# Mixing stage of a gMLP-and-attention kernel: three accumulations opened on six blocks, the last two blocks after all three, and one operand prepared earlier

## The chip, the cores and the metric

The kernel runs on one core of a Trainium2 chip. A core has TensorE (PE, the matmuls; PEld are its weight loads), VectorE (DVE), ScalarE (ACT), GpSimd (POOL), and SyncE (SP), which issues most of the transfers. Each engine works through its own list of instructions in order and waits on semaphores for the others. The metric is device microseconds of one execution. Times inside the profile are us from the start of the span.

## The reference

```
xn = layernorm(x)                                   # x: 2048 x 512
s  = attention(xn, k_cache, v_cache, wq, wo)        # 32 heads of 128, the last 512 keys
z  = gelu(xn @ w_in)                                # w_in: 512 x 1376
z1, z2 = z[:, :688], layernorm(z[:, 688:])
g  = w_sp @ z2 + b_sp[:, None]                      # w_sp: 2048 x 2048, the "mixing"
out = x + s * silu((z1 * g) @ w_out)                # w_out: 688 x 512
```

All in float32.

## The kernel before

A float32 product is made of three matmuls. Each operand is split into a high half (a cast to fp32r on ACT) and a low half (whole minus high half, by `rest`, L59, on DVE or POOL); the three are high by high, high by low, low by high.

The program has three stretches: attention together with the z1 products (to about 1450 us), the z2 products with their gelu and layernorm (to about 1511 us), and then the mixing product w_sp @ z2 and the projection. The change lies where the second stretch meets the third.

**The z2 loop (L929 to L943).** It walks the 16 row blocks of z2 in the order `ZO` = 8, 9, 0, 1, 10, 11, 2, 3, 12, 13, 4, 5, 14, 15, 6, 7. At position `pos` it first splits the normed pair of rows that ended two positions before (`z_split`: cast L812 on ACT, low half L59 on POOL), then makes the products of this row block for both halves of the 688 columns, with gelu (L787, ACT) and statistics (L788, DVE); `z_norm` closes a layernorm for each pair (L794 on DVE, then L74, L75 and two L801 on POOL), and `z_apply` (L806, ACT, one for each row block of the pair) applies it one position later. Each position also runs `step(t)` with t = pos - 16.

**Slots.** The mixing product is done by a seven-product scheme on half-size blocks for each of the 8 row pairs. A slot (r, k) is one of these products: eight blocks along the contraction, three matmuls each, 24 matmuls (L870) into one bank `ps`. The operand that moves is a pair of z2 row blocks (`b`), the stationary one a prepared row of w_sp (`x8`, printed as x). Slots 0 to 3 are P2 of rows 0 to 3, slots 4 to 7 are P1 of rows 0 to 3. P2 moves B21, which is made of the z2 rows 8 to 15; its blocks seven and eight are rows 14 and 15, which stand at positions 12 and 13 of `ZO` and are split at position 15 (t = -1). P1 moves B11; its blocks seven and eight are rows 6 and 7, positions 14 and 15, applied at t = 1 and split at t = 2.

**Operands.** `prep(n)` prepares the stationary operand of slot n: a cast of 128x1024 on ACT (L855) and its low half on DVE (L59, with x in its names). prep(0) and prep(1) stand at t = -6 and t = -4; from then on `step(t)` starts with prep(t + 2). `step` then runs the events put down for t: `t_diff` (L884, DVE, in pairs) and `t_split` (L889 on ACT, L59 with b in its names on DVE) make the combinations of z2 that later slots move. The rows of w_sp come by `load_halves` (L828, issued by SP): P2 rows 2 and 3 at t = -4, P1 rows 0 and 1 at t = 0, P1 rows 2 and 3 at t = 2. All operands and loaded rows take turns in the eight buffers of the pool `xp`.

**The slot loop (L1097).** For each t it evicts slot t - 1 (P2: nothing; P1: L990 on ACT, L991 and L975 on DVE), runs step(t), and then products(t).

Of the kernel before, what the change touches and what calls it, by code (L numbers as in the profile page):

```python
# [23 lines left out]
NB = FH // 2  # L24
# [16 lines left out]
def mixer_kernel(ctx: ExitStack, tc: tile.TileContext, x, wh, w_in, w_sp, b_sp, w_out, out):  # L41
# [218 lines left out]
    def fetch_x(w, k):  # L260
        X[w][k] = block()
        nc.sync.dma_start(X[w][k].bitcast(F32), xd[w, k])
# [89 lines left out]
    def z1_product(i, n, between=lambda: None):  # L352
        ps = ps_acc.tile([P, 512], F32, name="ps_a") if n or i >= T8 else ps_step.tile([P, 512], F32, name="ps_3")
        zmm(ps[:, :NB], i, n, range(2))
        between()
        zmm(ps[:, :NB], i, n, range(2, NC))
        return ps
# [255 lines left out]
    n, t = 0, 28  # L613
    for p in range(4):
        seq, store = later_x(p)
        for k, (f, ks) in enumerate(seq):
            t = max(t + 2, 30 + 13 * n // 5)
# [43 lines left out]
    ps = ps_step.tile([P, 512], F32, name="ps_3")  # L661
# [9 lines left out]
    ps = ps_step.tile([P, 512], F32, name="ps_3")  # L671
# [4 lines left out]
    ps = ps_acc.tile([P, 512], F32, name="ps_a")  # L676
# [18 lines left out]
    for t in range(T0, T1):  # L695
# [30 lines left out]
        if t in DRAIN:  # L726
            ps = z1_product(*DRAIN[t])
# [21 lines left out]
    ps = z1_product(*LAST[-1])  # L749
# [5 lines left out]
    RP = NT // 2  # L755
# [14 lines left out]
    def hilo(k, j, pool=None):  # L770
        if pool is not None:
            HL[k, j] = blk(pool)
        return tuple(HL[k, j][:, a, :, :NB] for a in range(2))
# [5 lines left out]
    def z_product(i, n):  # L779
        last = i in ZO[-2:]  # L780
        zps[i, n] = (ps_step if last else ps_acc).tile([P, 512], F32, name="ps_3" if last else "ps_a")
        zmm(zps[i, n][:, :NB], i, n, range(NC))

    def z_gelu(i, n):
        if n == 2:
            zst[i] = stats.tile([P, 2, 6], F32, name="stz")
        nc.scalar.activation(zt(i)[:, n - 2], zps[i, n][:, :NB], AF.Gelu_apprx_tanh)  # L787
        nc.vector.bn_stats(zst[i][:, n - 2, :], zt(i)[:, n - 2])  # L788

    def z_norm(pos):  # L790
        g, j = divmod(pos, 2)
        if j == 0:
            zmv[g] = stats.tile([P, 2, 2], F32, name="mvz")
        nc.vector.bn_aggr(zmv[g][:, j, :], zst[ZO[pos]])  # L794
        if j == 1:
            r = stats.tile([P, 2], F32, name="rz_r")
            tmp = stats.tile([P, 2], F32, name="rz_t")
            rsqrt(zmv[g][:, :, 1], r, 2, tmp)
            for k in range(2):
                t, mean, rs = zt(ZO[pos - 1 + k]), zmv[g][:, k, 0:1], r[:, k:k + 1]  # L800
                nc.gpsimd.tensor_scalar(tmp[:, k:k + 1], mean, rs, -1.0, op0=OP.mult, op1=OP.mult)  # L801
                zn.setdefault(pos, []).append((t, tmp[:, k:k + 1], rs))

    def z_apply(pos):
        for t, shift, rs in zn.pop(pos, ()):
            nc.scalar.activation(t, t, AF.Identity, bias=shift, scale=rs)  # L806

    def z_split(pos):
        i = ZO[pos - 1]
        hi, lo = hilo("B21" if i >= RP else "B11", i % RP // 2, br)  # L810
        whole = Z[i // 2][:, :, 0, :NB]
        nc.scalar.copy(hi, whole)  # L812
        rest(nc.gpsimd, lo, whole, hi)
# [6 lines left out]
    NS = len(SLOTS)  # L820
    WHEN = {s: n for n, s in enumerate(SLOTS)}

    rows, s1, ops, bank = {}, {}, {}, {}
# [22 lines left out]
    def prep(n, engine):  # L846
        r, k = SLOTS[n]
        if k in ("P2", "P1"):
            src = rows[k, r // 2][:, r % 2]
        else:  # L850
            a11, a12, a21, a22 = a_blocks(r)
            src = {"P6": a11, "P5": s1[r], "P7": a21, "P3": a12, "P4": a22}[k]
        op = ops[n] = x8([P, 2, RP, P])
        hi, lo = (op[:, a].rearrange("p c t -> p (c t)") for a in range(2))
        nc.scalar.copy(hi, src)  # L855
        rest(engine, lo, src, hi)

    MOVING = {"P1": "B11", "P2": "B21", "P6": "T2", "P5": "T1", "P7": "T3", "P3": "B22", "P4": "T4"}

    def products(n):  # L860
        r, k = SLOTS[n]
        if k == "P4":
            bank[r, k] = bank.pop((r, "P7"))
        else:
            bank[r, k] = pp.tile([P, 512], F32, name="ps", bufs=6)
        ps, op = bank[r, k][:, :NB], ops.pop(n)
        for c in range(RP):
            rh, rl = (t[:, c % 2] for t in hilo(MOVING[k], c // 2))
            for m, (a, b) in enumerate(((op[:, 0, c], rh), (op[:, 0, c], rl), (op[:, 1, c], rh))):
                nc.tensor.matmul(ps, a, b, start=k != "P4" and c == 0 and m == 0,  # L870
                                 stop=c == RP - 1 and m == 2, skip_group_check=True)
# [25 lines left out]
    V, G = nc.vector, nc.gpsimd  # L897

    def step(t):
        if 1 < t + 2 < NS:  # L900
            prep(t + 2, V)
        for f, args in ev.get(t, ()):
            f(*args)
# [25 lines left out]
    for pos, i in enumerate(ZO):  # L929
        if pos > 2 and pos % 2:  # L930
            z_split(pos - 2)
        for n in (2, 3):
            z_product(i, n)
            z_gelu(i, n)
        z_norm(pos)
        z_apply(pos - 1)
        if pos == 5:
            for k in ((0, 1), (1, 1)):
                fetch_x(0, k)
        t = pos - NT  # L940
        if t in (-6, -4):
            prep(t // 2 + 3, nc.vector)
        step(t)  # L943
    left.close()
# [35 lines left out]
    def evict(r, k):  # L980
        if k == "P2":
            return
        ps = (bank[r, k] if k == "P7" else bank.pop((r, k)))[:, :NB]
        v = us[r][:, 3 * NB:4 * NB] if r in us else None
        if k == "P1":
            if r % 4 == 0:
                t = blk(br, F32).rearrange("p a c f -> p (a c f)")
                U.update({r + n: t[:, n * ZW:n * ZW + NB] for n in range(4)})
            c = bank.pop((r, "P2"))[:, :NB]
            nc.scalar.copy(U[r], ps)  # L990
            nc.vector.tensor_tensor(c, c, U[r], op=OP.add)  # L991
            gate(r, 0, c)
        elif k == "P6":
            nc.vector.tensor_tensor(U[r], ps, U[r], op=OP.add)
        elif k == "P5":
            nc.vector.tensor_tensor(v, ps, U[r], op=OP.add)
        elif k == "P7":
            g = pp.tile([P, 512], F32, name="ps_f")[:, :NB]
            nc.vector.tensor_tensor(g, ps, v, op=OP.add)
            gate(r + RP, 1, g)  # L1000
        elif k == "P3":
            nc.vector.tensor_tensor(ps, ps, v, op=OP.add)
            gate(r, 1, ps)
        else:
            nc.vector.tensor_tensor(ps, ps, U[r], op=OP.add)
            gate(r + RP, 0, ps)
# [90 lines left out]
    for t in range(NS):  # L1097
        if t:
            evict(*SLOTS[t - 1])
        step(t)  # L1100
        products(t)
    evict(*SLOTS[NS - 1])
    for t in (NS, NS + 1):
        for f, args in ev.get(t, ()):
# [57 lines left out]
```

## Time and profile before

| what | value |
|---|---|
| median of 3 runs (lowest, highest) | 1793.61 us (1790.58, 1795.43) |
| the profiled execution | 1795.06 us, its span 1793.2 us |
| PE busy | 1770.9 us, 99% of the span |
| DVE, POOL, ACT busy | 1484.6, 1260.9, 1184.5 us |
| mean granted clock of TensorE | 0.996 |
| L870, products of the slots | 1344 matmuls, from 1511.1 to 1727.0 us |

PE is busy nearly all the time, so an idle stretch of PE, or a stretch at a lower granted clock, is what can be had. A matmul's duration overlaps the next one's, so the pace is read from starts and counts and not from durations.

### The profile page before, as it was taken

To read this page: it belongs to the slowest core of one execution; us is meant where nothing else is said; L and a number is where in the kernel's file an instruction comes from. 1 tells how busy PE (TensorE), PEld (TensorE's weight loads), DVE (VectorE), ACT (ScalarE), POOL (GpSimd) and SP (SyncE) were. 2 spreads that over 40 slices of the span, in tenths; PEclk is the share of its full clock that TensorE was granted. 3 is DMA by queue.
4 is the path that set the end of the run, shared out by engine and by line. 5 is a ranking of instruction groups with operands and counts; after the bars stand their busy time and mean duration, and the time that the engine had idled before them with its cause. 6 is when DMAs were issued, how large, how long until landed. Compare 5 with 4: busy or idle time off the path is not lost.

```text
span 1793.2 us, 28567 instructions
## 1 busy us (share of the span) xinstructions
PE 1770.9 (99%) x8460; PEld 1516.4 (85%) x8460; DVE 1484.6 (83%) x2442; ACT 1184.5 (66%) x2634; POOL 1260.9 (70%) x1204
## 2 busy tenths in 40 slices
PE   8999999999999999899999999999999999999999
PEld 7888888888888887688888888888888999999997
DVE  5689988989898988788888888888889646787776
ACT  4777777777777776577777777777777546543333
POOL 2798898898898987678888888888888425000033
PEclk9999999999999999999999999999999999999999
DMA  5588887987888989787787777777778752555487
GB/s 189 182 246 233 244 264 230 265 253 232 256 252 240 268 233 285 237 262 229 221 233 221 224 222 233 221 220 222 230 221 256 213 193 87 196 183 175 146 243 212
DMA packets 181164, 402.12 MB, mean 224 GB/s; under 512 B 24080, under 2 KB 61200, under 8 KB 161808
## 3 DMA queue, kind: packets, MB, share of 16 engines
q1 hardware_dynamic: 176400, 394.66, 74.2%
q10 hardware_dynamic: 4608, 5.64, 0.9%
q8 instruction: 66, 1.08, 0.3%
q14 instruction: 90, 0.74, 0.1%
HBM read 233.74 MB, written 166.46 MB: 223 GB/s over the span
## 4 chain that ended last, share of the span: by engine, by line
PE 88%; DMA 5%; DVE 3%; POOL 2%; ACT 1%; issue 1%; SPq 1%; ACTq 0%; DVEq 0%; POOLq 0%
PE ps_a L450 14%; PE ps L870 12%; PE ps L67 12%; PE ps L65 12%; PE ps L66 12%; PE ps_a L517 6%; PE ps_a L515 6%; PE ps_a L516 6%; PE ps_a L67 2%; PE ps_a L65 2%; PE ps_a L66 2%; DMA p_dram<-pL 1%; DMA pL<-p_dram 1%; PE ps_f L65 1%; PE ps_f L67 1%
## 5 line engine op out<-in xcount | busy, mean ns | idle before, releaser
L59 POOL TENSOR_TENSOR pT_l<-pL,pT_h 128x512 fp32r<-128x512 f32 x507 | 657.2, 1300 | 189.0 <-ACT pT_h L507 179.0
L479 ACT ACTIVATE prob<-ps,nm 128x512 f32<-128x512 f32 x512 | 354.0, 691 | 338.8 <-DVE nm L477 331.1
L539 DVE SCALAR_TENSOR_TENSOR sacc<-ps,sums,sacc 128x512 f32<-128x512 f32 x496 | 370.2, 747 | 129.9 <-PE ps L67 124.4
L450 PE MATMUL ps_a<-x,x 128*128 128x512 f32 x1302 | 377.3, 390 | 5.7 <-DMA x<-x_dram 5.6
L488 DVE STREAM_TRANSPOSE pL<-prob 128x512 f32<-128x512 f32 x512 | 359.4, 702 | 4.1 <-ACT prob L479 4.1
L477 DVE TENSOR_REDUCE nm<-ps 128x1 f32<-128x512 f32 x512 | 340.8, 666 | 6.5 <-PE ps L67 6.4
L507 ACT CAST pT_h<-pL 128x512 fp32r<-128x512 f32 x512 | 318.5, 622 | 21.8 <-DMA pL<-p_dram 14.3
L450 PEld LDWEIGHTS ps_a<-x,x 128*128 128x128 f32 x1302 | 244.5, 188 | 58.5 <-DMA x<-x_dram 5.5
L59 POOL TENSOR_TENSOR wl<-raw,wh 128x512 fp32r<-128x512 f32 x186 | 241.6, 1299 | 11.9 <-ACT wh L144 11.9
L870 PE MATMUL ps<-b,x 128*128 128x344 f32 x1344 | 214.2, 321 | 2.0 <-POOL b L59 1.3
L870 PEld LDWEIGHTS ps<-b,x 128*128 128x128 f32 x1344 | 213.6, 189 | 2.6 <-POOL b L59 1.5
L517 PE MATMUL ps_a<-pT_l,wh 128*128 128x512 f32 x512 | 200.1, 391 | 2.3 <-POOL pT_l L59 2.1
L515 PE MATMUL ps_a<-pT_h,wh 128*128 128x512 f32 x512 | 200.3, 391 | 0.5 <-ACT pT_h L507 0.5
L65 PE MATMUL ps<-wh,qT_h 128*128 128x512 f32 x512 | 199.9, 390 | 0.6 <-DVE sacc L539 0.6
L67 PE MATMUL ps<-wh,qT_l 128*128 128x512 f32 x512 | 200.0, 391 | 0.3
L66 PE MATMUL ps<-wl,qT_h 128*128 128x512 f32 x512 | 199.5, 390 | 0.0
L67 PE MATMUL ps<-wh,oT_l 128*128 128x512 f32 x512 | 199.5, 390 | 0.0
L65 PE MATMUL ps<-wh,oT_h 128*128 128x512 f32 x512 | 199.4, 390 | 0.0
L66 PE MATMUL ps<-wl,oT_h 128*128 128x512 f32 x512 | 199.4, 389 | 0.0
L516 PE MATMUL ps_a<-pT_h,wl 128*128 128x512 f32 x512 | 199.3, 389 | 0.0
L59 POOL TENSOR_TENSOR b<-b 128x688 fp32r<-128x688 f32 (+1 forms) x10 | 18.2, 1820 | 216.8 <-ACT b L1038 188.2
L59 POOL TENSOR_TENSOR x<-wq,x 128x256 fp32r<-128x256 f32 x186 | 138.2, 743 | 1.5 <-ACT x L432 1.5
(205 smaller groups left out, 3006.1 us busy)
## 6 DMA issues: line engine op xcount, KB each, us to landing
p_dram<-pL SPq DMA_DIRECT2D x128, 1024.0 KB, 4.8
pL<-p_dram SPq DMA_DIRECT2D x256, 192.0 KB, 4.0
raw<-wh SPq DMA_DIRECT2D x188, 256.0 KB, 6.2
pL<-p_dram SPq DMA_DIRECT2D x256, 128.0 KB, 3.9
x<-w_sp SPq DMA_DIRECT2D x24, 1024.0 KB, 5.2
pL<-p_dram SPq DMA_DIRECT2D x256, 64.0 KB, 3.9
wq<-wh SPq DMA_DIRECT2D x62, 256.0 KB, 5.7
x_dram<-rawx SPq DMA_DIRECT2D x32, 256.0 KB, 6.0
```

Source lines behind the costliest of these rows:

```text
L59: engine.tensor_tensor(lo, whole, hi.bitcast(F32), op=OP.subtract)
L65: nc.tensor.matmul(ps, lh, rh, start=first, stop=False)
L66: nc.tensor.matmul(ps, lh, rl, start=False, stop=False)
L67: nc.tensor.matmul(ps, ll, rh, start=False, stop=last)
L450: nc.tensor.matmul(qps[g, bank], wt["q", g, k][a][:, c * P:(c + 1) * P], X[g * 2 // H][ORDER[k]][:, b, c], start=first, stop=r == 5, skip_ ...
L477: nc.vector.tensor_reduce(nm, ps, axis=AX.X, op=OP.max, negate=True)
L479: nc.scalar.activation(prob[t], ps, AF.Exp, bias=nm, accum_out=sums[b][:, j:j + 1])
L488: nc.vector.transpose(pL[b][:, :, j * P:j * P + P].rearrange("p a (c q) -> p a c q", q=Q), prob.pop(t).rearrange("p (a c q) -> p a c q", a ...
L507: nc.scalar.copy(h, p)
L515: nc.tensor.matmul(pps[b], vh, ph, start=c == 0, stop=False)
L539: nc.vector.scalar_tensor_tensor(at, ps, rs, at, op0=OP.mult, op1=OP.add)
L870: nc.tensor.matmul(ps, a, b, start=k != "P4" and c == 0 and m == 0, stop=c == RP - 1 and m == 2, skip_group_check=True)
```

## The change

Three edits. `products` takes a range of blocks, opens the bank when the range starts at block 0 and drops the operand when it ends at the last block. The slot loop runs blocks one to six of slots 0, 1 and 2, and then blocks seven and eight of the three. prep(2) moves from the start of step(0) to position 14 of the z2 loop (t = -2), ahead of that position's events; step starts its own preps with slot 3.

```
-    def products(n):
+    def products(n, cs=range(RP)):
         r, k = SLOTS[n]
         if k == "P4":
             bank[r, k] = bank.pop((r, "P7"))
-        else:
+        elif cs[0] == 0:
             bank[r, k] = pp.tile([P, 512], F32, name="ps", bufs=6)
-        ps, op = bank[r, k][:, :NB], ops.pop(n)
-        for c in range(RP):
+        ps, op = bank[r, k][:, :NB], ops.pop(n) if cs[-1] == RP - 1 else ops[n]
+        for c in cs:
...
     def step(t):
-        if 1 < t + 2 < NS:
+        if 2 < t + 2 < NS:
             prep(t + 2, V)
...
-        if t in (-6, -4):
+        if t in (-6, -4, -2):
             prep(t // 2 + 3, nc.vector)
         step(t)
...
         step(t)
-        products(t)
+        if t > 2:
+            products(t)
+            continue
+        products(t, range(RP - 2))
+        if t == 2:
+            for n in range(3):
+                products(n, range(RP - 2, RP))
```

On PE, at the start of the slots, before (x_18619, x_18703, x_18847, x_18883 are the operands of slots 0 to 3):

```order
L870 MATMUL ps<-b,x_18619 128x344 x24
L870 MATMUL ps<-b,x_18703 128x344 x24
L870 MATMUL ps<-b,x_18847 128x344 x24
L870 MATMUL ps<-b,x_18883 128x344 x24
L870 MATMUL ps<-b,x_18921 128x344 x24
```

and now (the operands of slots 2, 3 and 4 are here x_18788, x_18877 and x_18909):

```order
L870 MATMUL ps<-b,x_18619 128x344 x18
L870 MATMUL ps<-b,x_18703 128x344 x18
L870 MATMUL ps<-b,x_18788 128x344 x18
L870 MATMUL ps<-b,x_18619 128x344 x6
L870 MATMUL ps<-b,x_18703 128x344 x6
L870 MATMUL ps<-b,x_18788 128x344 x6
L870 MATMUL ps<-b,x_18877 128x344 x24
L870 MATMUL ps<-b,x_18909 128x344 x24
```

The first matmul on blocks seven and eight was the 19th of the slots and is now the 55th; operand 2 was first read by the 49th and is now first read by the 37th.

On DVE, from the last statistics of position 14 to the operand of slot 4 (L884 are the pairs of t_diff, L788 and L794 the statistics of position 15, L59 with b the low halves of t_split):

```order
 L794 BN_AGGR mvz<-stz 128x2
+L59 TENSOR_TENSOR x_18788<-x_18706,x_18788 128x1024
 L884 TENSOR_TENSOR b<-b 128x2x344 x2
 L788 BN_STATS stz<-b 128x6 x2
 L794 BN_AGGR mvz<-stz 128x2
 L884 TENSOR_TENSOR b<-b 128x2x344 x2
-L59 TENSOR_TENSOR x_18847<-x_18706,x_18847 128x1024
 L59 TENSOR_TENSOR b<-b 128x2x344 x2
-L59 TENSOR_TENSOR x_18883<-x_18706,x_18883 128x1024
+L59 TENSOR_TENSOR x_18877<-x_18706,x_18877 128x1024
 L59 TENSOR_TENSOR b<-b 128x2x344 x2
```

The low half of operand 2 now stands ahead of the statistics of the last row block and of both L884 pairs, where it stood behind them. On ACT its cast moves in the same way: it now stands between L806 of rows 14 and 15 and the L812 that splits them, where it stood behind the last L787.

On SP, the loads of w_sp rows for P1 (rows 0 and 1, then 2 and 3) and for P2 of rows 4 and 5, with the semaphores that each waits for:

```order
 L828 DMA x_18850<-w_sp 128x2x1024 [waits DMAHW2_49,PE_49]
-L828 DMA x_18927<-w_sp 128x2x1024 [waits DMAHW4_49,DVE_49,PE_49]
-L828 DMA x_18996<-w_sp 128x2x1024 [waits DVE_49,PE_49]
+L828 DMA x_18915<-w_sp 128x2x1024 [waits DMAHW4_49,DMAHW1_49,DVE_49]
+L828 DMA x_18996<-w_sp 128x2x1024 [waits PE_49]
```

The load of P1 rows 2 and 3 (x_18927, now x_18915) waited for the last matmul of slot 0, whose operand's buffer it took. It now takes the buffer of the P2 rows 2 and 3 (x_18706) and waits for the low half of operand 3 on DVE, which reads them last.

## The prediction

> **What bounds the kernel now.** I read the page first, then PE's waits, then the place of the change in order of time. The page says that PE is the bound everywhere; only what PE loses can be won.
>
> ```profile
> span 1793.2 us, 28567 instructions
> PE 1770.9 (99%) x8460; PEld 1516.4 (85%) x8460; DVE 1484.6 (83%) x2442; ACT 1184.5 (66%) x2634; POOL 1260.9 (70%) x1204
> ```
>
> Of PE's waits, two belong to the slots' products (us in total, times, longest): 1.3 + 0.7 = 2.0 us.
>
> ```profile
> PE ps L870 <- POOL b L59: 1.3, 1, 1.3
> PE ps L870 <- ACT b L812: 0.7, 1, 0.7
> ```
>
> The order of time on PE puts both in slot 0, ahead of its 19th and 20th product, the first ones on block seven. After that nothing waits.
>
> ```profile
> 1511.06 2.92 PE L870 MATMUL ps<-b,x 128*128 128x344 f32 x18
> 1514.71 0.42 PE L870 MATMUL ps<-b,x 128*128 128x344 f32 x1 [0.73 <-ACT b L812]
> 1516.44 28.78 PE L870 MATMUL ps<-b,x 128*128 128x344 f32 x171 [1.31 <-POOL b L59]
> ```
>
> The granted clock (the number after the busy times) shows a second loss. Here is the stretch with the wait and the two that follow, each 3.41 us long, and three stretches around 738 us, where PE waits for a transfer:
>
> ```profile
> 1513.31:1516.72 3.41, 1.37 (x8) 0.86 (x7) 1.64 (x4) 3.38 (x6) 1.89 (x2) 1.00 0.15 57
> 1516.74:1520.15 3.41, 3.41 (x14) 3.41 (x13) 3.38 (x5) 1.95 (x4) 3.23 (x4) 0.50 0.28 53
> 1520.15:1523.56 3.41, 3.41 (x23) 3.41 (x23) 1.72 (x2) 2.46 (x4) 1.77 (x1) 1.00 0.64 255
> ...
> 735.08:738.49 3.41, 2.14 (x10) 1.42 (x8) 2.52 (x5) 1.26 (x3) 2.85 (x4) 1.00 1.03 218
> 738.49:741.90 3.41, 1.51 (x7) 1.25 (x8) 0.40 (x1) 1.92 (x4) 1.23 (x1) 1.00 0.88 339
> 741.91:745.32 3.41, 3.41 (x10) 2.64 (x9) 1.97 (x3) 1.02 (x4) 3.23 (x4) 0.50 0.37 96
> ```
>
> A stretch in which PE was idle for 3.41 - 1.37 = 2.04 us, or 1.90 us, was followed by one at clock 0.50; one with 1.27 us idle was not. So the wait costs 2.04 us and then half of 3.41, 1.71 us: 3.75 us in all, 0.21% of the span. A measurement of this kernel tells about 0.3% (5.4 us) from no change, so even the whole prize lies below that.
>
> The Trainium skill ("TensorE: Matmul & The Clock Gate", Part 1, "What's actually happening") has the clock fall to half after at least one idle window of about 3.4 us. By that rule 2.04 us of idle time would cost only themselves; the 0.50 row speaks against it, and the measurement decides.
>
> **PE's side of the change.** The pace of the slots comes from one row (first and last start):
>
> ```profile
> L870 PE MATMUL ps<-b,x x1344: 314/320/492, 1511.1 to 1727.0; 128*128 128x344 f32 x192
> ```
>
> (1727.0 - 1511.1 - 3.75) / 1343 = 0.158 us a product, 3.79 us a slot. No product is added or removed. Now 54 products come before block seven: it is needed at 1511.06 + 54 x 0.158 = 1519.6. Operand 2's low half is needed by the 39th product: 1517.1. If neither is late, slots 0 to 2 end at 1522.4 and the two waits are gone. For comparison later: the 171-row's last product starts at 1545.22 - 0.32 = 1544.9, and the third product of slot 7 lies 19 products ahead of it, at 1541.9.
>
> **ACT and POOL's side.** The moved cast (1.03 us) now stands ahead of L812. The same sequence, cast, L812, low half of the block on POOL, stands in the trace once already, for prep(1):
>
> ```profile
> 1494.91 1.03 ACT L855 CAST x<-x 128x1024 fp32r<-128x1024 f32 x1
> 1511.98 1.88 ACT L806 ACTIVATE b<-b,rz_t,rz_r 128x688 f32<-128x688 f32 x2 [2.43 <-POOL rz_t L801]
> 1513.89 0.76 ACT L812 CAST b<-b 128x688 fp32r<-128x688 f32 x1
> 1514.56 0.80 ACT L787 ACTIVATE b<-ps 128x344 f32<-128x344 f32 x2
> 1521.95 0.96 ACT L806 ACTIVATE b<-b,rz_t,rz_r 128x688 f32<-128x688 f32 x1 [0.95 <-POOL rz_t L801]
> ```
> ```profile
> 1496.70 2.03 POOL L59 TENSOR_TENSOR b<-b 128x688 fp32r<-128x688 f32 x1 [4.26 <-ACT b L812]
> 1516.47 0.72 POOL L74 TENSOR_SCALAR rz_t<-mvz 128x2 f32<-128x2 f32 x1
> 1517.28 1.32 POOL L75 TENSOR_TENSOR rz_r<-rz_t,power 128x2 f32<-128x2 f32 x1
> 1518.69 3.23 POOL L801 TENSOR_SCALAR rz_t<-mvz,rz_r 128x1 f32<-128x1 f32 x2
> 1525.94 2.06 POOL L59 TENSOR_TENSOR b<-b 128x688 fp32r<-128x688 f32 x1 [4.03 <-ACT b L812]
> ```
>
> L806 ends at 1513.86, the cast at 1514.8, L812 at 1515.6, the low half on POOL (2.03 as at 1496.70) at 1517.7. Needed at 1519.6: 1.9 us to spare. The gelu L787 ends about 1 us later than before, at 1516.3.
>
> **DVE's side, where I expect the loss.**
>
> ```profile
> 1495.98 1.23 DVE L59 TENSOR_TENSOR x<-x,x 128x1024 fp32r<-128x1024 f32 x1 [1.80 <-ACT x L855]
> 1497.12 3.25 DVE L884 TENSOR_TENSOR b<-b 128x688 f32<-128x688 f32 x2
> ...
> 1511.00 1.73 DVE L884 TENSOR_TENSOR b<-b 128x688 f32<-128x688 f32 x2
> 1515.05 0.94 DVE L788 BATCH_NORM_STATS2 stz<-b 128x6 f32<-128x344 f32 x2 [2.32 <-ACT b L787]
> 1516.02 0.21 DVE L794 BATCH_NORM_AGGREGATE mvz<-stz 128x2 f32<-128x12 f32 x1
> 1516.14 1.89 DVE L884 TENSOR_TENSOR b<-b 128x688 f32<-128x688 f32 x2
> ...
> 1519.08 1.65 DVE L59 TENSOR_TENSOR b<-b 128x688 fp32r<-128x688 f32 x2
> 1520.65 1.22 DVE L59 TENSOR_TENSOR x<-x,x 128x1024 fp32r<-128x1024 f32 x1
> ...
> 1525.23 1.23 DVE L59 TENSOR_TENSOR x<-x,x 128x1024 fp32r<-128x1024 f32 x1
> ...
> 1529.44 1.21 DVE L59 TENSOR_TENSOR x<-x,x 128x1024 fp32r<-128x1024 f32 x1
> ...
> 1533.05 1.22 DVE L59 TENSOR_TENSOR x<-x,x 128x1024 fp32r<-128x1024 f32 x1
> ...
> 1538.53 1.22 DVE L59 TENSOR_TENSOR x<-x,x 128x1024 fp32r<-128x1024 f32 x1
> ...
> 1541.49 1.22 DVE L59 TENSOR_TENSOR x<-x,x 128x1024 fp32r<-128x1024 f32 x1
> ```
>
> The rows at 1520.65, 1525.23, 1529.44, 1533.05, 1538.53 and 1541.49 are the low halves of operands 3 to 8. In the two idle microseconds ahead of 1515.05 there is room for the moved low half, but it can't start there: its cast ends at 1514.8 only, and meanwhile the L884 pair that ran at 1511.00 is held behind it. So DVE now does from 1514.85 on: low half of operand 2 to 1516.1 (needed at 1517.1, met), L884 pair, statistics, L884 pair, two L59 b, low half of operand 3. The first pair is the one unknown. Alone it took 1.73 us; right behind the same cast and POOL's L59, at 1497.12, it took 3.25. I take 3.25, since the order around it on ACT, DVE and POOL is the same as there, and keep 1.73 as the other end. Then, with successive instructions overlapping by about 0.1 us: pair to 1519.25, statistics to 1520.3 (were done at 1516.23), second pair to 1522.1, the two L59 b to 1523.7, operand 3 to 1524.75. PE wants it, as the third product of slot 3, at 1522.4 + 0.3 = 1522.7: a new wait of 2.0 us.
>
> The statistics are also the start of the last layernorm. POOL's L74 and L75 (0.72 and 1.32) run to 1522.4, and the L801 pair, which before ended at 1521.92, just as DVE fell idle at 1521.87, would again end when DVE does, at about 1524.8. From the second L806 on, the same instructions follow in the same order as before, later by 1524.8 - 1521.95 = 2.85 us. So the low halves of operands 4, 5, 6, 7 and 8 are ready at 1529.3, 1533.5, 1537.1, 1542.6 and 1545.6. PE's third product of slot 4 could start at 1524.75 + 3.79 = 1528.5 and waits 0.8; slot 5 then 0.4; slot 6 (1537.3) not; slot 7 (1541.1) waits 1.5; slot 8 (1546.4) not, and from there the low halves gain on PE.
>
> The last POOL half, for P1's block seven (it ended at 1528.0), shifted by 2.85 too, is ready at 1530.85, and PE, 16 products after the third of slot 4, wants it at 1529.3 + 2.5 = 1531.8: no wait. The load on SP that now waits for operand 3 goes out near 1524.8, where it went out at 1518.04:
>
> ```profile
> 1518.04 0.37 SPq L828 DMA_DIRECT2D x<-w_sp  x1
> DMA to landing us min/median/max: 5.0/5.2/6.9
> ```
>
> It lands by 1524.8 + 6.9 = 1531.7 at the latest, and the operand made of it (slot 6) is cast behind 1532; the P2 load queued behind it on SP isn't wanted until slot 8. I cost both at nothing; if the load took 5 us longer, slot 6 would wait about as long.
>
> **Sum.** The third product of slot 7 starts at 1542.6 instead of 1541.9: +0.7 us (waits and half clock removed 3.75, new waits 2.0 + 0.8 + 0.4 + 1.5 = 4.7, the quarter of a us between the two is the rounding of the pace). With the pair at 1.73 the chain is 1.5 us earlier and the sum is -0.8. The profiled execution took 1795.06 us (1793.2 of span), 1.45 above the median of the runs; I put the sum on the median: 1793.61 + 0.7 = 1794.3.
>
> **Rivals.**
>
> *Most of the gain stays.* The low halves come no later than before. For it: DVE idled 2.32 us ahead of the row at 1515.05, and one low half less now lies behind the statistics. Against: between 1514.85 and the end of operand 3 DVE has 8.4 us of work even with the short pair, and PE leaves it 7.85. Even with no lateness at all operand 7, ready at 1538.53 + 1.22 = 1539.75, holds slot 7 to a gain of 1541.9 - 1539.75 = 2.15: 1791.5. The whole 3.75, 1789.9, would need the chain 1.6 us earlier than before.
>
> *The clock turns the new waits into a real loss (slower).* Place: slots 3 to 7. If one 3.41 us stretch holds more than between 1.27 and 1.90 us of idle PE, the next runs at 0.50 and costs 1.71 us. Slot 3's wait of 2.0 and slot 7's of 1.5 are near that border. One such stretch gives 1796.0, two 1797.7; beyond 0.3% it gets only with three, 1799.4.
>
> *The half clock of before isn't in the timed runs.* If a border of the stretches falls into the 2.04 us of idle time, no stretch holds enough of it. Then before loses 2.04 only, the profiled row being one case, and the sum is 0.7 + 1.7 = +2.4: 1796.0. The skill's rule above would give the same.
>
> *It does not do what it says.* The halves of blocks seven and eight come later than 1519.6, because ACT's cast or POOL is held up by over 1.9 us. PE then waits there, the chain stays as it is: about 1795.
>
> **Chances.** New waits eat the gain: 0.50. Most of the gain stays: 0.20. Clock: 0.13. No half clock before: 0.10. Not what it says: 0.07. The likeliest gives 1794.3, its own range is 1792.8 (short pair) to 1796.0. The range from the whole gain, 1789.9, to two half-clock stretches, 1797.7, leaves out 0.1 or less, and some of the spread of the runs (4.85 us between lowest and highest). Faster by over 0.3%: 0.03, since 3.75 is short of 5.4 and only spread could carry it; slower: 0.05, the clock rival's end; within: 0.92.
>
> **What would show it.** In the changed kernel's PE waits, L870 no longer waits for L812 or for POOL's L59; it waits for DVE's L59 (the low halves) in slots 3, 4 and 7, 3 to 5 us together. On DVE the L884 pair behind operand 2 takes about 3.25 us, and operand 3's low half ends near 1524.75, operand 7's near 1542.6. The clock shows no 0.50 at 1517. I am wrong if no L870 wait is left and slot 8 starts 2 us or more sooner, or if a 0.50 row follows slot 3 or slot 7.

## The result and the profile after

The changed kernel takes 1796.88 us (median of 10 runs, 1794.42 to 1801.15), the kernel before 1792.47 us (10 runs, 1788.51 to 1796.03): ratio 1.0027, 95% interval 1.0015 to 1.0039. It is slower by 4 to 5 us (0.27%; the interval reaches from 0.15 to 0.39%), clear of noise and by its middle just inside the 0.3% that I had called no change. The profiled execution took 1801.15 us, its span:

```profile
span 1799.4 us, 28565 instructions
PE 1774.0 (99%) x8460; PEld 1519.0 (84%) x8460; DVE 1486.0 (83%) x2442; ACT 1184.0 (66%) x2634; POOL 1259.4 (70%) x1204
```

PE's waits in the slots (us in total, times, longest), and the products in order of time:

```profile
PE ps L870 <- ACT b L990: 3.0, 1, 3.0
...
PE ps L870 <- ACT b L787: 1.8, 1, 1.8
...
PE ps L870 <- DVE x L59: 0.6, 1, 0.6
```
```profile
1511.98 2.92 PE L870 MATMUL ps<-b,x 128*128 128x344 f32 x18
1516.65 12.92 PE L870 MATMUL ps<-b,x 128*128 128x344 f32 x80 [1.75 <-ACT b L787]
1530.19 7.92 PE L870 MATMUL ps<-b,x 128*128 128x344 f32 x46 [0.62 <-DVE x L59]
1541.16 19.01 PE L870 MATMUL ps<-b,x 128*128 128x344 f32 x102 [3.05 <-ACT b L990]
```

The waits for blocks seven and eight (L812 and POOL's L59) are gone. Three others stand in their place: ahead of product 19 (the first of slot 1), product 99 (18 + 80 + 1, the third of slot 4) and product 145 (18 + 80 + 46 + 1, the first of slot 6). With 0.13 us in slot 5 they make 5.55 us, where before had 2.04. Then the clock (after the busy times, as in the prediction):

```profile
1512.95:1516.36 3.41, 1.95 (x13) 1.68 (x11) 0.74 (x1) 3.41 (x5) 0.11 (x2) 1.00 0.51 186
1516.36:1519.78 3.42, 3.12 (x20) 3.13 (x21) 3.38 (x3) 2.86 (x5) 2.02 (x1) 1.00 0.00 0
...
1536.85:1540.26 3.41, 1.26 (x8) 0.97 (x7) 3.38 (x4) 1.50 (x2) 0.00 (x0) 1.00 0.47 178
1540.26:1543.67 3.41, 2.51 (x9) 2.51 (x10) 2.67 (x5) 3.41 (x6) 0.00 (x0) 0.50 0.00 0
1543.67:1547.08 3.41, 3.41 (x14) 3.41 (x14) 2.67 (x4) 0.35 (x1) 0.00 (x0) 0.50 0.81 214
```

The wait of slot 6 is followed by two stretches at half clock. PE was busy for 2.51 + 3.41 us of them, and half of that is lost, 2.96 us, where before lost 1.71. So: 5.55 + 2.96 = 8.51 us against 2.04 + 1.71 = 3.75, a loss of 4.8 us. Counting products in the trace in order, from the first of slot 0 to the first of slot 8, slots 0 to 7 took 34.3 us before and 39.5 after, 5.2 us more; from there to the last slot product it is 181.6 us in both. The 0.4 us between 4.8 and 5.2 fits what the starts behind a wait show: the two products behind the 1.75 us wait start 2.07 and 0.26 us after the one ahead of each, 0.26 us more than the wait and twice the pace of 0.158, and there are four waits where there were two. The whole loss lies in slots 0 to 7. (The span differs by 0.9 us more; the first slot product already starts 0.9 us later, at 1511.98.)

Where the waits come from is seen on ACT and DVE. First ACT after the change, then the two rows of before that answer to its last ones:

```profile
1514.55 1.03 ACT L855 CAST x<-x 128x1024 fp32r<-128x1024 f32 x1
1515.49 0.76 ACT L812 CAST b<-b 128x688 fp32r<-128x688 f32 x1
1516.16 0.79 ACT L787 ACTIVATE b<-ps 128x344 f32<-128x344 f32 x2
...
1538.76 0.77 ACT L889 CAST b<-b 128x688 fp32r<-128x688 f32 x1 [3.82 <-DVE b L884]
1539.43 1.34 ACT L962 ACTIVATE x<-x 128x1376 f32<-128x1376 f32 x1
1540.68 0.43 ACT L990 COPY b<-ps 128x344 f32<-128x344 f32 x1
```
```profile
1535.09 0.77 ACT L889 CAST b<-b 128x688 fp32r<-128x688 f32 x1 [3.82 <-DVE b L884]
...
1537.02 0.42 ACT L990 COPY b<-ps 128x344 f32<-128x344 f32 x1
```

The moved cast at 1514.55 pushes L812 and the last gelu L787 back, the gelu by 0.7 us when the shift of the start (0.92) is taken off (before it stood at 1514.56). Slot 1 now begins 18 products after slot 0 and not 24 products and two waits after it; its bank is the one from which that gelu reads the last row block's first half, so PE waits for it, 1.75 us. There are six banks named `ps` (a bank holds the sums of one slot); slots 0 to 3 keep theirs until P1 of the same row is added, so slot 6 needs the bank of slot 4, and L990, which evicts slot 4, frees it. On ACT it stands behind L889, which waits for an L884 on DVE, and behind L962. It ran at 1537.02 before and runs at 1540.68 now, 2.7 us later when the shift of the start is taken off. On DVE:

```profile
1515.62 1.23 DVE L59 TENSOR_TENSOR x<-x,x 128x1024 fp32r<-128x1024 f32 x1 [3.61 <-ACT x L855]
1516.76 3.27 DVE L884 TENSOR_TENSOR b<-b 128x688 f32<-128x688 f32 x2
...
1520.91 0.21 DVE L794 BATCH_NORM_AGGREGATE mvz<-stz 128x2 f32<-128x12 f32 x1
...
1524.26 1.22 DVE L59 TENSOR_TENSOR x<-x,x 128x1024 fp32r<-128x1024 f32 x1
...
1528.91 1.23 DVE L59 TENSOR_TENSOR x<-x,x 128x1024 fp32r<-128x1024 f32 x1
...
1542.19 1.22 DVE L59 TENSOR_TENSOR x<-x,x 128x1024 fp32r<-128x1024 f32 x1
```

The L884 pair behind the moved low half takes 3.27 us, and everything from the last layernorm on follows late, as the prediction had it.

### The profile page after: what moved, and what is told of

It is laid out like the page before. It is cut to its first block, busy times and chain, and to the rows that moved or that the text cites. A ratio compares the mean times of both kernels' runs of the same rounds, so it can differ in the third digit from the quotient of the medians.

```text
span 1799.4 us, 28565 instructions
## 1 busy us (share of the span) xinstructions
PE 1774.0 (99%) x8460; PEld 1519.0 (84%) x8460; DVE 1486.0 (83%) x2442; ACT 1184.0 (66%) x2634; POOL 1259.4 (70%) x1204
## 4 chain that ended last, share of the span: by engine, by line
PE 90%; DVE 3%; ACT 2%; DMA 2%; POOL 1%; issue 1%; SPq 0%; ACTq 0%; DVEq 0%; POOLq 0%
PE ps_a L450 15%; PE ps L67 12%; PE ps L65 12%; PE ps L66 12%; PE ps L870 11%; PE ps_a L517 6%; PE ps_a L515 6%; PE ps_a L516 6%; PE ps_a L67 2%; PE ps_a L66 2%; PE ps_a L65 2%; PE ps_f L67 1%; PE ps_f L65 1%; PE ps_f L66 1%; DMA x<-x_dram 1%
## 5 line engine op out<-in xcount | busy, mean ns | idle before, releaser
L59 POOL TENSOR_TENSOR pT_l<-pL,pT_h 128x512 fp32r<-128x512 f32 x507 | 657.3, 1300 | 189.0 <-ACT pT_h L507 178.5
L59 POOL TENSOR_TENSOR wl<-raw,wh 128x512 fp32r<-128x512 f32 x186 | 241.5, 1299 | 13.4 <-ACT wh L144 13.4
L870 PE MATMUL ps<-b,x 128*128 128x344 f32 x1344 | 215.9, 322 | 5.5 <-ACT b L990 3.0
L59 POOL TENSOR_TENSOR b<-b 128x688 fp32r<-128x688 f32 (+1 forms) x10 | 18.5, 1857 | 220.7 <-ACT b L1038 190.7
L59 POOL TENSOR_TENSOR x<-wq,x 128x256 fp32r<-128x256 f32 x186 | 138.2, 744 | 1.5 <-ACT x L432 1.5
```

What stands on the lines that cost most here:

```text
L59: engine.tensor_tensor(lo, whole, hi.bitcast(F32), op=OP.subtract)
```

## Experiments

Two theories at first. A: the moved cast and low half make ACT and DVE late, and two waits for PSUM banks show it (PSUM is the memory of the banks `ps` and `ps_f`). B: the new order of blocks does the harm, because PE reaches banks that aren't free. Each kernel was timed against the kernel before in the same session.

**The two parts apart.** The changed kernel with operand 2 prepared where it was before:

```
-        if 2 < t + 2 < NS:
+        if 1 < t + 2 < NS:
...
-        if t in (-6, -4, -2):
+        if t in (-6, -4):
```

> The new order of blocks for slots 0 to 2 alone; the operand of slot 2 is prepared where it was before. The eight slots 0 to 7 took 34.3 us of PE before and 39.5 after the change. Theory A (the moved cast and low half make ACT and DVE late, and two waits for PSUM banks show it): slot 1's first product waits 1.1 us for the last gelu, which frees its bank (1.75 after the change), slot 2's third about 0.9 us for its operand's low half, slot 6's first about 1.5 us for L990 (3.05 after the change), because L990 stands where it stood before; slots 0 to 7 take 34 us, one half-clock stretch at the most on top; time within 0.1% of before. Theory B (the order of blocks does the harm, since PE reaches banks that are not free): slots 0 to 7 take 38 us or more, about 4 us slower than before.

```profile
PE ps L870 <- ACT b L990: 1.3, 1, 1.3
PE ps L870 <- ACT b L787: 1.1, 1, 1.1
PE ps L870 <- DVE x L59: 0.8, 1, 0.8
```

1791.73 us against 1792.01: ratio 0.9994 (0.9986 to 1.0003). Slots 0 to 7 took 34.1 us, with no half clock. The three waits are those that A named, each within 0.3 us. The block order alone does no harm, but it wins nothing either: 3.1 us of wait stand where 2.0 us and 1.7 us of half clock stood.

The kernel before with only the preparation moved (the same two edits the other way round):

> The operand of slot 2 prepared two positions sooner, blocks in the order of before. Theory A: PE waits longer in slot 0 than before, about 1.5 us for L812 and 1.9 us for POOL's low half, then a half-clock stretch; L990 comes about 3 us later than before, and slot 6's first product waits about 1.2 us for it; slots 0 to 7 take 36.7 us, up to 38.4 with a second half-clock stretch (34.3 before), 2.4 to 4 us slower. Theory B (the moved preparation is harmless, the block order costs): 34.3 us or less, as before.

```profile
PE ps L870 <- POOL b L59: 1.7, 1, 1.7
PE ps L870 <- ACT b L812: 1.4, 1, 1.4
PE ps L870 <- ACT b L990: 1.2, 1, 1.2
```
```profile
1510.33 3.23 DVE L884 TENSOR_TENSOR b<-b 128x688 f32<-128x688 f32 x2
```
```profile
1534.22 0.43 ACT L990 COPY b<-ps 128x344 f32<-128x344 f32 x1
```

1793.53 us, ratio 1.0007 (0.9998 to 1.0015). In the trace slots 0 to 7 took 36.8 us, 2.5 us more than before, with one half-clock stretch; the times show 1.5 us more at the medians, with no change just inside the interval, and so less than the 2.4 to 4 us that A gave. The slow L884 pair is there again (3.23 us), so it comes with the moved preparation; why the pair is slow there stays open. The trace decides for A, where the times alone would not.

The loss of the whole change is more than that of its parts, because the block order brings PE to slot 6 earlier and the moved preparation frees its bank later. Counted from the first slot product of each trace, L990 ends at 26.4 us before and with the block order alone, and at 29.1 us with the preparation alone and in the changed kernel: here 1534.22 + 0.43 - 1505.55 = 29.1.

**Fewer slots opened.** Blocks one to six of slots 0 and 1 only, preparation as before (`products` takes a range of blocks as in the changed kernel):

```
         step(t)
-        products(t)
+        if t > 1:
+            products(t)
+            continue
+        products(t, range(RP - 2))
+        if t == 1:
+            for n in range(2):
+                products(n, range(RP - 2, RP))
```

> Blocks one to six of slots 0 and 1 only, then their blocks seven and eight, slot 2 whole behind them, its operand prepared as before. Theory A: slot 1's first product waits 1.1 us for the last gelu, no wait on blocks seven and operand 2, and slot 6's first product waits about 2.5 us for L990, which stands as before: slots 0 to 7 take 34.0 us, or 35.7 if that wait halves the clock; so time as before or up to 1.5 us more: what is won in slot 0 is given back at slot 6's bank. Theory B: also slower by some us, by waits at slot 1. A third possibility, that the wait at slot 6 is of the change's own making and not there without the moved operand: slots 0 to 7 take 31.5 us, 2.8 us faster.

```profile
PE ps L870 <- ACT b L990: 2.3, 1, 2.3
PE ps L870 <- ACT b L787: 1.1, 1, 1.1
```
```profile
1535.45 0.42 ACT L990 COPY b<-ps 128x344 f32<-128x344 f32 x1
```

1791.02 us, ratio 0.9997 (0.9986 to 1.0009). Slots 0 to 7 took 35.5 us with one half-clock stretch, as expected for the second branch. So the wait at slot 6's bank is there without the moved operand: L990 ends 1535.45 + 0.42 - 1509.48 = 26.4 us after the first slot product, the same as before, and what PE wins earlier it gives back there.

**The bank of slot 6.** The changed kernel, with slots 6 and 7 in the two banks of ps_f, idle at that time:

```
-            bank[r, k] = pp.tile([P, 512], F32, name="ps", bufs=6)
+            bank[r, k] = pp.tile([P, 512], F32, name="ps_f") if n in (6, 7) else pp.tile([P, 512], F32, name="ps", bufs=6)
```

> The changed kernel, with slots 6 and 7 accumulating in the two banks that stand idle until the seventh product of row 0 (the ps_f banks), so that slot 6 needn't wait for slot 4's bank. Theory A: the 3.05 us wait for L990 is gone, slot 7's third product now waits about 1.2 us for its operand's low half on DVE, no half clock near slot 6; slots 0 to 7 take 34 us instead of 39.5, time about 5 us below the changed kernel's and equal to before. If not the bank but the late operands hold slots 6 and 7 anyway: 37 us or more, within 2 us of the changed kernel.

```profile
PE ps L870 <- ACT b L787: 1.7, 1, 1.7
PE ps_f L870 <- DVE x L59: 0.8, 1, 0.8
PE ps L870 <- DVE x L59: 0.6, 1, 0.6
PE ps_f L870 <- ACT x L855: 0.2, 1, 0.2
```

1791.73 us, ratio 0.9994 (0.9986 to 1.0003), where the changed kernel stands at 1.0027 (1.0015 to 1.0039): one line that moves two accumulators takes the whole loss back. The 3.05 us wait and the half clock behind it are gone; slot 7 now waits 1.0 us for its operand (0.2 for the cast, 0.8 for the low half), where the prediction's chain had 1.5. Slots 0 to 7 took 35.1 us, 0.7 more than before: with that one bank out of the way the trace shows the sum of the prediction, though its waits stand in part at other places.

**A second effect.** The trace with two opened slots held a surprise. Its slot products behind the wait at slot 6 start closer together than in every other trace. Here are the products that start between 1600 and 1700 us (x count: duration min/median/max in ns), in the kernel before, the changed kernel, and the one with two opened slots:

```profile
L870 PE MATMUL ps<-b,x x636: 317/320/321, 1599.8 to 1700.0; 128*128 128x344 f32 x159
```
```profile
L870 PE MATMUL ps<-b,x x636: 317/320/321, 1599.8 to 1700.0; 128*128 128x344 f32 x159
```
```profile
L870 PE MATMUL ps<-b,x x654: 316/316/316, 1599.8 to 1699.9; 128*128 128x344 f32 x164
```

That is 100.2 / 635 = 157.8 ns from start to start against 100.1 / 653 = 153.3 ns, at granted clock 1.00 in all three, on the same instructions. And in every trace the 18 products ahead of the first wait of the stage (2.92 us with the last one's 0.32) run at (2.92 - 0.32) / 17 = 153 ns. So I set up a kernel without any wait in slots 0 to 8: the kernel with two opened slots, with slot 1 and slot 6 in the banks of ps_f, the products with the operand's low half put behind the others of blocks one to six in slots 2 to 9, operand 7 prepared right behind operand 6, and one t_split later.

```
-            bank[r, k] = pp.tile([P, 512], F32, name="ps", bufs=6)
+            bank[r, k] = pp.tile([P, 512], F32, name="ps_f") if n in (1, 6) else pp.tile([P, 512], F32, name="ps", bufs=6)
...
+        order = [(c, m) for c in cs for m in range(3)]
+        if 1 < n < 10:
+            order = [(c, m) for c in range(6) for m in (0, 1)] + [(c, 2) for c in range(6)] + order[18:]
...
-        if 1 < t + 2 < NS:
+        if 1 < t + 2 < NS and t != 5:
             prep(t + 2, V)
+        if t == 4:
+            prep(7, V)
...
-        on((0, 1, 2, 5)[j], t_split, j, "T1", V)
+        on((0, 1, 2, 8)[j], t_split, j, "T1", V)
```

> All waits of slots 0 to 8 taken away: slots 0 and 1 opened on six blocks with operand 2 prepared as before, slot 1 in an idle bank (ps_f) that the last gelu doesn't hold, slot 6 in the other, the products with the low half of the operand put last in slots 2 to 9, operand 7 prepared right behind operand 6, one t_split (T1 of the last pair) moved from t = 5 to t = 8. Theory A1 (a wait costs its length and at most one half-clock stretch): slots 0 to 7 take 30.3 us (34.3 before), the last slot product starts 212 us after the first (215.9 before), time about 4 us (0.22%) below before. Theory A2 (a wait also changes the pace of all products behind it: in the traces the 18 products ahead of the first wait start 153.3 ns apart, those behind it 157.7, and in the kernel with two opened slots 153.3 again behind the wait at slot 6): without any wait all 1344 products keep 153.3 ns, slots 0 to 7 take 29.4 us, the last slot product starts 206 us after the first, time about 10 us (0.55%) below before.

```profile
L873 PE MATMUL ps<-b,x x1296: 316/316/316, 1507.7 to 1713.7; 128*128 128x344 f32 x186
```

1782.12 us (5 runs), ratio 0.9939 (0.9925 to 0.9952), its slowest run (1783.57) below the fastest of before (1789.05). It beats both kernels. No wait of a slot product is left, slots 0 to 7 took 29.4 us, and the last slot product starts 205.9 us after the first, as A2 said. Of the 10.0 us that the stage lost before, 2.04 were wait, 1.71 half clock and the rest, about 6, the pace behind the wait.

The same kernel with slot 1 back in the bank that the last gelu holds (slots 6 and 7 in ps_f):

```
-            ... if n in (1, 6) else ...
+            ... if n in (6, 7) else ...
```

> The kernel without waits, but slot 1 in the bank that the last gelu frees, so that its first product waits about 1.1 us; slots 6 and 7 in the idle banks. Theory A1: 1.1 us above the kernel without waits. Theory A2: behind that wait the products start 157.7 ns apart, 4.4 ns more for 1326 products: 1.1 + 5.8 = about 7 us above the kernel without waits; last slot product 213 us after the first.

```profile
PE ps L873 <- ACT b L787: 1.1, 1, 1.1
```
```profile
L873 PE MATMUL ps<-b,x x636: 317/320/321, 1599.7 to 1699.9; 128*128 128x344 f32 x159
```

1790.24 us, ratio 0.9989 (0.9980 to 0.9998): 8 us above the kernel without waits for a wait of 1.1 us; the last slot product starts 213.2 us after the first.

Last, one wait put in far from the change, in the kernel without waits:

```
-        if 1 < t + 2 < NS and t != 5:
+        if 1 < t + 2 < NS and t != 5 and t + 2 not in (13,):
             prep(t + 2, V)
...
+        if t in (13,):
+            prep(t, V)
```

> The kernel without waits, with one wait put in far behind the change: operand 13 is prepared at step 13, behind the eviction of slot 12, and not at step 11, so that PE waits 2 to 2.5 us at slot 13. Theory A1 (the pace belongs to the place or the banks): the products start 153.3 ns apart before and behind that wait; time 2 to 4 us above the kernel without waits. Theory A2 (the wait changes the pace): 153.3 ns up to slot 12, 157.7 from slot 13 to the last slot, 43 slots x 24 x 4.4 ns = 4.5 us more; time 6.5 to 9 us above the kernel without waits. Since one wait in the kernel with two opened slots went back to 153.3, a look that stays at 153.3 wouldn't refute A2 alone; the times of the other runs would then have to spread over both.

```profile
1531.55 22.24 PE L873 MATMUL ps<-b,x 128*128 128x344 f32 x144
1559.61 0.94 PE L873 MATMUL ps<-b,x 128*128 128x344 f32 x2 [5.81 <-ACT x L855]
1560.87 164.63 PE L873 MATMUL ps<-b,x 128*128 128x344 f32 x1030 [0.32 <-DVE x L59]
```

1796.54 us, ratio 1.0023 (1.0012 to 1.0034). The 144 products ahead of the wait run at (22.24 - 0.32) / 143 = 153.3 ns, and in the trace each slot behind slot 13 runs at 157.7. The wait was 6.1 us, not the 2 to 2.5 that I expected, and the clock was halved for 6.83 us, of which PE was busy for 5.09. So 6.1 + 2.5 + 4.5 for the pace = 13.1 us; from the first slot product to the last it is 219.4 us, 13.5 more than without waits, and the medians, of two sessions, lie 14.4 apart. Why the operand came so late I did not follow up.

And with `(10, 13)` in place of `(13,)` in both lines:

> As the kernel with the wait at slot 13, with operand 10 also prepared two steps later. Nothing on ACT's list ahead of it waits for PE there, so I expect no wait at slot 10 or a short one, and a second look at the pace behind a wait at slot 13: A2 157.7 ns, A1 153.3.

A single run, 1803.23 us. My expectation for slot 10 was wrong: it waited 7.8 us for its cast. The pace was 153.3 ns up to slot 9 and 157.7 from slot 10 on, behind both waits.

## Why the prediction was right or wrong

The time (1794.3, range 1789.9 to 1797.7; measured 1796.88) and the sign of the sum were right; the change was too small: 0.7 us said, 4.4 measured between the medians of one session. There is luck in the time. The likeliest case had a range of its own, up to 1796.0, and the measured time lies above it. And the forecast started from 1793.61, the median of three runs, where ten runs gave 1792.47; with the measured 4.4 us on the first it would be 1798.0, outside the whole range. The total of the waits, 4.7 us said and 5.55 measured, agrees by chance, since most of it stood at other places for other reasons.

*The chain on DVE was right, to a quarter of a us.* Taking 0.92 off the times after for the later start: the pair took 3.27 us (3.25 taken from the one row like it), the low half of operand 3 was ready at 24.26 + 1.22 - 0.92 past 1500 = 1524.6 (1524.75 said), of operand 4 at 1529.2 (1529.3), of operand 7 at 1542.5 (1542.6). That is the part on which the forecast that new waits eat the gain rested, and the preparation moved alone shows that the slow pair comes with it.

*The first edit's own aim was right.* Blocks seven and eight were no longer waited for.

*The places of the waits were wrong, since two waits for PSUM banks were missing.* I followed only operands and blocks. As a sign I had named 3 to 5 us of waits for DVE's low halves in slots 3, 4 and 7; they were 0.62 + 0.13 us, in slots 4 and 5, and the banks took 1.75 + 3.05. The step "slots 0 to 2 end at 1522.4" left out that slot 1's bank is held by the last gelu; PE lost 1.75 us there, and because of that the 2.0 us that I had put at slot 3 never showed: operand 3 was as late as I said, and PE later still. The step "slot 6 (1537.3) not" left out that slot 6's bank is freed by L990. In the profile of before there is no such wait, but there is the row: L990 ended at 1537.44 and slot 6 began, 45 products ahead of 1544.9, at 1537.8. A third of a us was all that this stage had to spare: whatever was won in slot 0, PE could not start slot 6 sooner by more than that. The experiment with two opened slots shows just that, and the one with other banks shows that without this wait the loss is gone. The 1.5 us that I had put at slot 7 stood behind it, hidden; 1.0 showed with other banks.

*The clock rival came true in its price and not in its cause.* I gave two half-clock stretches 1797.7 and the whole rival a chance of 0.13. Two came, but behind the wait for slot 6's bank, which the rival didn't have, and not behind slot 3 or slot 7.

*The size of the prize was wrong.* That "even the whole prize lies below that", below 0.3%, took the pace of 0.158 us as given, from (1727.0 - 1511.1 - 3.75) / 1343. The quoted row of 18 products in 2.92 us says 0.153 for the same instructions ahead of the wait. The whole prize was 0.6%, as the kernel without waits shows (it has more edits than this change); I averaged over the very effect that made the wait dear.

## What to carry to other kernels

Before moving work to close a wait, list every resource that the released engine meets next, PSUM banks and recycled buffers among them, with the time by which each is free today: a margin of a third of a us shows in no list of waits, and it caps the gain. A preparation moved ahead on an engine's list delays all that stands behind it on that list; what the first L884 pair took behind the same neighbours in another place was the best price for it. And compare the pace of equal instructions ahead of a wait and behind it, for the wait may cost more than its length.

## What the runs showed of the hardware

*The pace behind a wait.* In these traces the slot products run at one of two paces, 153.3 or 157.7 ns from start to start at granted clock 1.00, and keep it until the next wait. Without a wait all 1344 kept 153.3; behind a wait of 1.1 us, of 5.8 and of 7.8 it was 157.7, for up to 200 us. Behind the second wait of the kernel with two opened slots, 2.3 us with a half-clock stretch, it was 153.3 again, while the same wait at 1.2 to 1.3 us in the two kernels with one part of the change left 157.7. That a wait changes the pace is shown; what chooses between the two stays open. So does how often each comes, for there is one trace of each kernel: with two opened slots the traced stage was 3.9 us shorter than before (212.0 against 215.9), yet the medians of the runs differ by 1.0 us only, and the single runs reach from 1784.57 to 1794.30. The Trainium skill ("TensorE: Matmul & The Clock Gate", Part 2, "Back-to-back issue gap") gives an isolated gap of columns / 2.4 + 2.5 ns, by which 145.8 would be the estimate for 344 columns, and says that in a stream the weight loads have a part in the spacing. Both paces measured here are above that estimate, and it doesn't tell them apart.

*The clock.* A stretch of 3.41 us with 1.90 us or more of idle PE was followed by one at 0.50, one with 1.46 us (3.41 - 1.95 in the rows after) was not, and neither was one with 1.74 us in the kernel with other banks (1508.51 to 1511.92). Behind 2.15 us of idle time the half clock held for two stretches, the first of which had 0.90 us of idle time itself.
